# Decode attention: projection weights in runs of four rows, the head dimension ordered by ScalarE during the PSUM copy, the last tile's columns placed by TensorE

## The chip, the cores and the metric

The kernel runs on one core of one Trainium2 chip. The metric is the device time of one execution in microseconds (us). Medians are quoted with the number of runs. The runs are on several chips, so every kernel is compared with runs of the kernel before in the same rounds on the same chip. A ratio is the mean time of one kernel's runs over that of the other's runs of the same rounds, so it isn't quite the ratio of the medians that stand beside it. A profile is one execution; its span is about 1.8 us shorter than the time of the same run.

The engines are TensorE (PE in the profile, PEld for its weight loads), VectorE (DVE), ScalarE (ACT) and SyncE (SP), which issues the DMAs, all but three of 10 KB or less.

## The reference

One token of each of 8 sequences attends to a cache of 4096 keys in 32 heads of 128, and a small MLP runs on the doubly normalised input. Only the attention matters here:

```python
x = A_x                                      # [8, 1, 640] bf16
xn = _layernorm(x)
q = (xn @ wq)            # -> [b, h, 1, 128]
scores = einsum("bhqd,bhkd->bhqk", q, k_cache) * 128**-0.5
o = einsum("bhqk,bhkd->bhqd", softmax(scores), v_cache)
attention = o.reshape(8, 1, 4096) @ wo       # wo [4096, 640]
return x + attention + MLP(layernorm(xn))
```

The caches are 537 MB together; everything else is about 15 MB.

## The kernel before

The work is cut into 64 tiles: a quad of 4 heads of one sequence. A tile needs 4 MB of keys (K) and 4 MB of values (V). Two K and two V buffers are filled in turn by one DMA queue. For each tile VectorE computes three quarters of q·K (multiply L558, fold L562, reduce L565, each twice), TensorE with ScalarE the rest. The softmax runs once per group of two tiles, except in the last group, where it runs per tile. Then TensorE multiplies with V into `PV_ps`, ScalarE copies that from PSUM to SBUF (`E_sb`, "the eviction"), TensorE turns it into columns (`OT_ps`), VectorE divides by the row sums and puts the columns where the projection wants them ("the placement"), and TensorE projects with `wo_sb`.

`wo_sb` holds `RW` consecutive rows of the projection weights in each partition. The larger `RW`, the longer the pieces that the DMA reads, but the head dimension must then be put into another order, and a column must be cut into `RW` blocks of partitions that VectorE moves to other partitions. `RW` is 2 before. TensorE makes the order by reading V with stride 2.

```python
RW, PB = 2, P // 2
...
wov = wo_sb[:, :, :].rearrange("p (y r) n -> p y (r n)", r=RW)
...
def vcols(t):
    return KV_sb[:, NK + t % NV, :].rearrange("p (j q r) -> p j r q", q=PB, r=RW)
...
def wo_rows(src):                                   # pieces of RW rows: 2560 bytes
    return src.rearrange("(y p r) n -> p y (r n)", p=P, r=RW)
... # values(t): the products with V, 32 matmuls of 128x512
r = e.matmul(PV_ps[32 * ct:32 * ct + HT * 4, t % 2, :], P_sb[:, i, m, :, :]...,
             vv[:, 4 * m:4 * m + 4, :, :], start=(q == 0), stop=(q == wide - 1))
... # the eviction: contiguous on both sides (L649)
e.activation(E_sb[:, k, 0:n], PV_ps[:, k, 0:n], ACT.Copy)
... # finish(g): the placement, 4 operations of 64x4 per group (L679)
for x in range(RW):
    for r in range(RW):
        q = slice(r * PB, (r + 1) * PB)
        i = e.tensor_tensor(dst[x * PB:(x + 1) * PB, r::RW, b0:b0 + GT],
              OT_ps...[q, x::RW, :], rinv_sb[q, g % 2, :]...[:, x::RW, :], ALU.mult)
...
def pe_keep(e, n):   # n dummy matmuls that keep TensorE busy near the end
    ...
for pos, n in ((pvpos(T - 2) + 0.25, 2), (pvpos(T - 1) + 0.075, 4), (pvpos(T - 1) + 0.115, 3), (pvpos(T - 1) + 0.2, 1)):
    add("pe", pos, lambda e, n=n: pe_keep(e, n), ...)
```

The last tile's V comes in three pieces (half, quarter, quarter), so that its product can start before all of it is there.

## Time and profile before

| | before |
|---|---|
| time, median of 3 runs | 1290.28 us (1290.17 to 1290.29) |
| span of the profiled run | 1288.2 us |
| load queue busy | 99.8% of 16 engines |
| VectorE busy | 89% |
| one 4 MB load lands after the one before | 9.71 us |
| VectorE waits for K | 51.8 us in all |

From the page of the profiled run: the busy time of each engine, the load queue, and the chain of work that ended last, by engine.

```profile
PE 641.0 (50%) x7931; PEld 403.3 (31%) x7934; DVE 1141.1 (89%) x680; ACT 496.9 (39%) x1243; POOL 0.2 (0%) x4
...
q1 hardware_dynamic: 21440, 551.80, 99.8%
...
DMA 77%; DVE 11%; PE 8%; issue 4%; ACT 0%; SPq 0%; DVEq 0%
```

The queue is never empty and the chain is DMA for three quarters of the span.

VectorE reaches the K of tile 4 10.4 us after it has landed. It gains on the DMA (149.2 us per eight tiles against 157.1, from the starts of L558 and the landings), has caught up at tile 13, and from there on waits for K once per group. This is the timeline of VectorE at the end of a group in the steady part (start us, us, engine, line, operation, names, shapes, count, and the idle time before with its cause):

```profile
920.04 0.68 DVE L679 TENSOR_TENSOR oTn_sb<-C_ps,rinv_sb 64x4 bf16<-64x4 f32 x4
921.72 3.36 DVE L558 TENSOR_TENSOR Y_sb<-KV_sb,qbc_sb 128x6144 bf16<-128x6144 bf16 x1 [0.99 <-DMA KV_sb<-in_A_k_cache_dram]
```

The four placements take 0.68 us together, and the wait behind them is the slack. The eviction is cheap (groups by shape; busy us and mean ns of one, then the idle time before):

```profile
L649 ACT ACTIVATE E_sb<-PV_ps 128x512 bf16<-128x512 f32 x64 | 38.2, 597 | 306.2 <-PE PV_ps L630 306.2
L649 ACT ACTIVATE E_sb<-PV_ps 128x128 bf16<-128x128 f32 x1 | 0.3, 278 | 2.0 <-PE PV_ps L640 2.0
```

The end of the chain, in order of time (start us, us, what):

```profile
1267.14 15.92 DMA KV_sb<-in_A_v_cache_dram
...
1283.11 0.74 PE PV_ps L640 x32
...
1283.86 0.29 ACT E_sb L649
...
1284.20 0.19 PE C_ps L662
...
1285.15 0.73 PE TR_ps L691 x8
...
1285.90 0.48 DVE out_sb L805
```

The last piece of V lands at 1283.06 us, and only 5.1 us of work follow it. All the other work of the last two tiles is done by then.

### The profile page before, as it was taken

Reading aid. Unit: us, or ns where it says so; the run is one execution under the profiler, and the core shown is the slowest. Engines: PE = TensorE matmul, PEld = TensorE weight load, DVE = VectorE, ACT = ScalarE, POOL = GpSimd, SP = SyncE. Lnnn points to the kernel's source line nnn. Section 1 sums busy time; section 2 is a strip of 40 time slices with the busy share of each in tenths; the row PEclk is TensorE's granted clock in tenths of the full one; section 3 lists DMA queues with packets and bytes.
Section 4 is the critical chain, followed back from the end, with each engine's and each line's share of the span. In section 5 each row is a group of like instructions: output and inputs, shape, how many; then the busy total and the mean of one; then the engine's idle time right before and its main releaser. Section 6 shows DMA issues by size and latency. Waiting matters only on the chain.

```text
span 1288.2 us, 19951 instructions
## 1 busy us (share of the span) xinstructions
PE 641.0 (50%) x7931; PEld 403.3 (31%) x7934; DVE 1141.1 (89%) x680; ACT 496.9 (39%) x1243; POOL 0.2 (0%) x4
## 2 busy tenths in 40 slices
PE   2754454444554455454455444544544554455456
PEld 1433233223333233232233232332332332333332
DVE  4989999998898898898988988988989989889895
ACT  1444344334344234343243342443432443433432
POOL 0000000000000000000000000000000000000000
PEclk9755555565555655656656556555565556655556
DMA  9999999999999999999999999999999999999998
GB/s 408 423 427 429 437 429 432 429 429 433 431 431 432 432 428 434 429 433 429 431 431 432 430 428 436 429 433 429 430 432 432 430 435 429 428 434 430 432 430 351
DMA packets 21488, 552.00 MB, mean 429 GB/s; under 512 B 2313, under 2 KB 2401, under 8 KB 4450
## 3 DMA queue, kind: packets, MB, share of 16 engines
q1 hardware_dynamic: 21440, 551.80, 99.8%
q8 instruction: 8, 0.13, 0.0%
q14 instruction: 6, 0.05, 0.0%
q10 hardware_dynamic: 34, 0.02, 0.0%
HBM read 551.80 MB, written 0.01 MB: 428 GB/s over the span
## 4 chain that ended last, share of the span: by engine, by line
DMA 77%; DVE 11%; PE 8%; issue 4%; ACT 0%; SPq 0%; DVEq 0%
DMA KV_sb<-in_A_v_cache_dram 73%; PE PV_ps L630 7%; DVE Y_sb L558 6%; DVE Y_sb L562 3%; DMA KV_sb<-in_A_k_cache_dram 2%; DVE S_sb L565 2%; DMA KV_sb<-in_A_wq_dram 2%; DVE oTn_sb L679 0%; DVE M_sb L577 0%; PE CH_ps L579 0%; SPq L372 0%; DVE rinv_sb L611 0%; PE PV_ps L640 0%; PE TR_ps L691 0%; PE TR_ps L470 0%
## 5 line engine op out<-in xcount | busy, mean ns | idle before, releaser
L558 DVE TENSOR_TENSOR Y_sb<-KV_sb,qbc_sb 128x6144 bf16<-128x6144 bf16 x128 | 429.0, 3352 | 67.0 <-DMA KV_sb<-in_A_k_cache_dram 51.8
L565 DVE TENSOR_REDUCE S_sb<-Y_sb 128x48 f32<-128x3072 bf16 x128 | 429.2, 3353 | 4.4
L529 ACT ACTIVATE KT_sb<-TR_ps 128x1024 bf16<-128x1024 bf16 x256 | 254.6, 1021 | 232.5 <-PE TR_ps L526 231.1
L630 PE MATMUL PV_ps<-KV_sb,P_sb 128*16 128x512 bf16 x2040 | 222.0, 609 | 132.0 <-DMA KV_sb<-in_A_v_cache_dram 132.0
L526 PE MATMUL TR_ps<-ident_bf,KV_sb 128*128 128x128 bf16 x2048 | 248.3, 308 | 53.1 <-DMA KV_sb<-in_A_k_cache_dram 52.6
L562 DVE TENSOR_TENSOR Y_sb<-Y_sb 128x3072 bf16<-128x3072 bf16 x128 | 225.0, 1758 | 4.4
L526 PEld LDWEIGHTS TR_ps<-ident_bf,KV_sb 128*128 128x128 bf16 x2048 | 200.4, 141 | 63.3 <-DMA KV_sb<-in_A_k_cache_dram 57.5
L536 PE MATMUL S_ps<-qk_sb,KT_sb 128*128 128x4 bf16 x2048 | 98.0, 170 | 140.3 <-ACT KT_sb L529 138.3
L649 ACT ACTIVATE E_sb<-PV_ps 128x512 bf16<-128x512 f32 (+1 forms) x65 | 38.5, 592 | 308.2 <-PE PV_ps L630 306.2
L536 PEld LDWEIGHTS S_ps<-qk_sb,KT_sb 128*128 128x128 bf16 x2048 | 85.9, 109 | 171.7 <-ACT KT_sb L529 171.7
L630 PEld LDWEIGHTS PV_ps<-KV_sb,P_sb 128*16 128x16 bf16 x2040 | 60.7, 120 | 246.3 <-DMA KV_sb<-in_A_v_cache_dram 137.2
L597 ACT ACTIVATE P_sb<-S_sb,NB_sb 32x128 bf16<-32x128 f32 x256 | 101.9, 398 | 3.8
L655 PE MATMUL C_ps<-sel_bf,E_sb 128*128 128x4 bf16 x256 | 16.9, 172 | 159.7 <-DVE rinv_sb L611 133.7
L591 ACT ACTIVATE NB_sb<-CH_ps 128x2 f32<-128x2 f32 (+1 forms) x33 | 5.7, 172 | 177.1 <-PE CH_ps L587 177.1
L579 PE MATMUL CH_ps<-ident_f,M_sb 128*2 128x128 f32 (+1 forms) x33 | 12.2, 369 | 117.7 <-DVE M_sb L577 117.7
L655 PEld LDWEIGHTS C_ps<-sel_bf,E_sb 128*128 128x128 bf16 x256 | 11.4, 103 | 189.4 <-DVE rinv_sb L611 136.4
L546 ACT ACTIVATE S_sb<-S_ps 32x32 f32<-32x32 f32 x256 | 48.2, 188 | 32.0 <-PE S_ps L536 29.8
L597 ACT ACTIVATION_READ_ACCUMULATOR P_sb<-S_sb,NB_sb 32x1 f32 x256 | 47.1, 184 | 0.0
L579 PEld LDWEIGHTS CH_ps<-ident_f,M_sb 128*2 128x2 f32 (+1 forms) x33 | 2.6, 80 | 120.6 <-DVE M_sb L577 120.6
L673 DVE MEMSET oTn_sb<- 128x16 uint32 x30 | 2.2, 72 | 31.1 <-PE ACC_ps L704 31.1
L581 DVE TENSOR_REDUCE M_sb<-CH_ps 2x4 f32<-2x128 f32 (+1 forms) x33 | 9.2, 279 | 15.9 <-PE CH_ps L579 15.9
L704 PE MATMUL ACC_ps<-oTn_sb,wo_sb 128*128 128x8 bf16 x600 | 20.8, 169 | 0.0
(96 smaller groups left out, 212.8 us busy)
## 6 DMA issues: line engine op xcount, KB each, us to landing
KV_sb<-in_A_k_cache_dram SPq DMA_DIRECT2D x64, 4096.0 KB, 26.8
KV_sb<-in_A_v_cache_dram SPq DMA_DIRECT2D x63, 4096.0 KB, 35.2
KV_sb<-in_A_wq_dram SPq DMA_DIRECT2D x1, 5120.0 KB, 23.8
wo_sb<-in_A_wo_dram SPq DMA_DIRECT2D x7, 640.0 KB, 30.8
KV_sb<-in_B_w_dram SPq DMA_DIRECT2D x1, 2160.0 KB, 39.0
w_sb<-in_B_w_dram SPq DMA_DIRECT2D x1, 2080.0 KB, 43.8
KV_sb<-in_A_v_cache_dram SPq DMA_DIRECT2D x1, 2048.0 KB, 12.7
KV_sb<-in_A_v_cache_dram SPq DMA_DIRECT2D x2, 1024.0 KB, 15.1
```

Source lines behind the costliest of these rows:

```text
L526: r = e.transpose(TR_ps[:, it.box[0], jj * P:(jj + 1) * P], kv[:, n * BK + jj, :], ident_bf[:, :])
L529: add("act", t - 0.59 + 0.12 * n, lambda e: e.activation(KT_sb[:, m % NS, :, :].rearrange("p a b -> p (a b)"), TR_ps[:, it.box[0], :], ACT ...
L536: r = e.matmul(S_ps[:, c:c + HT], KT_sb[:, m % NS, jj, :], qk_sb[:, :, i], start=True, stop=True)
L546: r = e.activation(S_sb[s, g % SR, i, 0:JP], S_ps[s, 0:JP * HT].rearrange("p (j a) -> p j a", a=HT)[:, :, a], ACT.Copy)
L558: return e.tensor_tensor(y, kv[:, j0:j1, :], qbc_sb[:, g % 2, i, :][:, None, :].to_broadcast([P, nj, P]), ALU.mult)
L562: lambda e, y=y, y2=y2: e.tensor_tensor(y2, y[:, :, 0:P // 2], y[:, :, P // 2:P], ALU.add),
L565: lambda e, y2=y2, j0=j0, j1=j1: e.tensor_reduce(S_sb[:, g % SR, i, j0:j1], y2, AX.X, ALU.add),
L597: r = e.activation(P_sb[s, i, :, a, :], S_sb[s, g % SR, i, :].rearrange("p (m c) -> p m c", c=4), ACT.Exp, bias=NB_sb[s, g % 2, i:i + 1], ...
L630: r = e.matmul(PV_ps[32 * ct:32 * ct + HT * 4, t % 2, :], P_sb[:, i, m, :, :].rearrange("p a c -> p (a c)"), vv[:, 4 * m:4 * m + 4, :, :], ...
L649: add("act", pos, lambda e: e.activation(E_sb[:, k, 0:n], PV_ps[:, k, 0:n], ACT.Copy), R=[("PV", k)] + ["wo"] * (t % GT and not last), W=[ ...
L655: r = e.matmul(OT_i, E_sb[:, t % 2, c * P:(c + 1) * P], sel_bf[:, c:HT * 4:4], start=(c == 0), stop=(c == 3 and not last))
L704: r = e.matmul(ACC_ps[:, c * B:(c + 1) * B], wo_sb[:, a, c * P:(c + 1) * P], oTn_sb[:, a, :], start=False, stop=False, skip_group_check=True)
```

## The change

The intent is longer DMA pieces (5120 bytes instead of 2560) and unit stride for TensorE's reads of V. The last quad keeps `LW = 2`, so that the work behind the last load stays short. ScalarE makes the order in the eviction. VectorE then has 4 x 4 = 16 placements of 32x2 per group in the first seven quads, 4 in the last. For the very last tile TensorE itself puts the columns into the right partitions with small matmuls, and VectorE needs one operation. Cut to its core:

```diff
-    RW, PB = 2, P // 2
+    RW, LW = 4, 2
-    def wo_rows(src):
-        return src.rearrange("(y p r) n -> p y (r n)", p=P, r=RW)
+    def wo_rows(src, w):
+        return src.rearrange("(y p r) n -> p y (r n)", p=P, r=w)
     ... # RW for the first seven loads, LW for the last quad's two
-            vv = vcols(t)
+            vv = vview(t)                      # unit stride
     ...
+            def ordered(ap, w):
+                return ap.rearrange("p (c r q) -> p c q r", r=w, q=P // w)
+            def natural(ap, w):
+                return ap.rearrange("p (c q r) -> p c q r", r=w, q=P // w)
             def evac(pos, k, n):
-                ... e.activation(E_sb[:, k, 0:n], PV_ps[:, k, 0:n], ACT.Copy)
+                if t < T - B:
+                    fn = lambda e: e.activation(ordered(E_sb[:, k, 0:n], RW), natural(PV_ps[:, k, 0:n], RW), ACT.Copy)
+                else:
+                    fn = lambda e: e.activation(ordered(E_sb[:, k, 0:n], LW), natural(PV_ps[:, k, 0:n], LW), ACT.Copy)
     ...
+            def pe_ex_last(e, k, sel, cs):     # the last tile: 16 and 4 small matmuls
+                ...
+                            i = e.matmul(OTL_ps[x * n:(x + 1) * n, r::LW], E_sb[:, k, c * P + r * n:c * P + (r + 1) * n],
+                                         sel[:, x * cs + c::LW * cs], ...)
     ...
-            def norm(e):
-                for x in range(RW):
-                    for r in range(RW): ...    # 4 of 64x4
+            def place(e, dst, w, gs):
+                for x in range(w):
+                    for r in range(w): ...     # 16 of 32x2 with w = RW, 4 with w = LW
+            ... # the last tile: one operation of 128x4 from OTL_ps, with rinvL_sb
```

Both views in the eviction walk in the order c, q, r. So PSUM is read contiguously, and the writes into `E_sb` are single bf16 elements, 32 elements apart with `RW` and 64 apart with `LW`. The change also moves the start of ScalarE's rolled loop (the part of its program that repeats every eight tiles) from 2.27 to 2.21.

More of the change, by code (lines that the diff above doesn't have):

```diff
@@ L287, in bass_parallel_sum__gqa_block_cached__mixer_channel_mlp__decode_kernel @@
         rinv_sb = sb("rinv_sb", [P, 2, HT * GT], F32)
+        rinvL_sb = sb("rinvL_sb", [P, HT // LW], F32)
         oTn_sb = sb("oTn_sb", [P, HT, B], BF)
@@ L300, in bass_parallel_sum__gqa_block_cached__mixer_channel_mlp__decode_kernel @@
         wov = wo_sb[:, :, :].rearrange("p (y r) n -> p y (r n)", r=RW)
+        wovL = wo_sb[:, :, :].rearrange("p (y r) n -> p y (r n)", r=LW)
         M1T_ps = CH_ps[0:GT, 0:P]
@@ L304, in bass_parallel_sum__gqa_block_cached__mixer_channel_mlp__decode_kernel @@
         RS_ps = C2_ps[:, 8:8 + HT * GT]
+        OTL_ps = C2_ps[:, 16:16 + HT]
+        RSL_ps = C2_ps[:, 20:20 + HT // LW]
         QB_ps = CH_ps[:, 2 * P:2 * P + GT * P]
@@ L327, in vview @@
             return KV_sb[:, NK + t % NV, :].rearrange("p (j d) -> p j d", d=P)
-        def vcols(t):
-            return KV_sb[:, NK + t % NV, :].rearrange("p (j q r) -> p j r q", q=PB, r=RW)
         def span(i, n):
@@ L401, in bass_parallel_sum__gqa_block_cached__mixer_channel_mlp__decode_kernel @@
         ld(-95.0, w2_sb[0:FR, FC, :], B_w2[FC * P:F, :], ["w2r"], "w2r")
-        def wo_rows(src):
-            return src.rearrange("(y p r) n -> p y (r n)", p=P, r=RW)
+        def wo_rows(src, w):
+            return src.rearrange("(y p r) n -> p y (r n)", p=P, r=w)
         for hg in range(NG - 1):
             ld(hg * B + 3.65, wov,
-               lambda hg=hg: wo_rows(A_wo[span(hg, HT * P), :]), ["wo"],
+               lambda hg=hg: wo_rows(A_wo[span(hg, HT * P), :], RW), ["wo"],
                "wo")
-        wo_last = wo_rows(A_wo[(H - HT) * P:H * P, :])
-        ld(T - 0.1, wov[:, 0:HT // RW - 1, :], wo_last[:, 0:HT // RW - 1, :], ["wo"], "wo")
-        ld(T - 0.09, wov[:, HT // RW - 1, :], wo_last[:, HT // RW - 1, :], ["wo3"], "wo3")
+        wo_last = wo_rows(A_wo[(H - HT) * P:H * P, :], LW)
+        ld(T - 0.1, wovL[:, 0:HT // LW - 1, :], wo_last[:, 0:HT // LW - 1, :], ["wo"], "wo")
+        ld(T - 0.09, wovL[:, HT // LW - 1, :], wo_last[:, HT // LW - 1, :], ["wo3"], "wo3")
         def layernorm(n, pos, src, src_res, dst, dst_res):
@@ L606, in rowsum @@
         def rowsum(g):
-            rp = pvpos(g * GT) + 0.21 if g < NGRP - 1 else pvpos(T - 1) - 0.04
+            rp = pvpos(g * GT) + 0.21
             add("pe", rp, lambda e: e.matmul(RS_ps, ones_f[:, :], rs_sb[:, :, :].rearrange("p a g -> p (a g)"),
@@ L612, in rowsum, with pe_rsl @@
                 R=["RS"], W=[("rinv", g % 2)], X=["C2"])
+            if g < NGRP - 1:
+                return
+            def pe_rsl(e):
+                n = P // LW
+                for x in range(LW):
+                    r = e.matmul(RSL_ps[x * n:(x + 1) * n, :], ones_f[:, 0:n], rs_sb[:, x::LW, GT - 1],
+                                 start=True, stop=True)
+                return r
+            add("pe", rp + .002, pe_rsl, R=[("rs", GT - 1), "ones"], W=["RSL"], X=["C2"])
+            add("dve", rp + .012, lambda e: e.reciprocal(rinvL_sb[:, :], RSL_ps), R=["RSL"], W=["rinvL"], X=["C2"])
         for g in range(NGRP):
@@ L631, in pe_pv @@
                                      P_sb[:, i, m, :, :].rearrange("p a c -> p (a c)"),
-                                     vv[:, 4 * m:4 * m + 4, :, :],
+                                     vv[:, 4 * m:4 * m + 4, :],
                                      start=(q == 0), stop=(q == wide - 1))
@@ L640, in pe_pv_last @@
                             r = e.matmul(PV_ps[32 * ct:32 * ct + HT, 1 - t % 2, 0:P], P_sb[:, i, m, :, c],
-                                         vv[:, 4 * m + c, :, :], start=(q == wide and c == 0),
+                                         vv[:, 4 * m + c, :], start=(q == wide and c == 0),
                                          stop=(q == NQ - 1 and c == 3))
@@ L646, in values @@
                     R=[("V", t % NV, q), ("Pt", i)], W=[("PV", k)], X=[("PVb", k)])
+            def ordered(ap, w):
+                return ap.rearrange("p (c r q) -> p c q r", r=w, q=P // w)
+            def natural(ap, w):
+                return ap.rearrange("p (c q r) -> p c q r", r=w, q=P // w)
             def evac(pos, k, n):
-                add("act", pos, lambda e: e.activation(E_sb[:, k, 0:n], PV_ps[:, k, 0:n], ACT.Copy),
+                if t < T - B:
+                    fn = lambda e: e.activation(ordered(E_sb[:, k, 0:n], RW), natural(PV_ps[:, k, 0:n], RW), ACT.Copy)
+                else:
+                    fn = lambda e: e.activation(ordered(E_sb[:, k, 0:n], LW), natural(PV_ps[:, k, 0:n], LW), ACT.Copy)
+                add("act", pos, fn,
                     R=[("PV", k)] + ["wo"] * (t % GT and not last), W=[("E", k)], X=[("PVb", k)])
@@ L655, in pe_ex @@
                     r = e.matmul(OT_i, E_sb[:, t % 2, c * P:(c + 1) * P], sel_bf[:, c:HT * 4:4],
-                                 start=(c == 0), stop=(c == 3 and not last))
+                                 start=(c == 0), stop=(c == 3))
                 return r
-            evac(p0 + (0.13 if last else 0.22), t % 2, 4 * P)
-            add("pe", p0 + (0.14 if last else 0.28), pe_ex, R=[("E", t % 2), "sel"], W=["OT"], X=["C2"])
-            if last:
+            def pe_ex_last(e, k, sel, cs):
+                n = P // LW
+                for r in range(LW):
+                    for c in range(cs):
+                        for x in range(LW):
+                            i = e.matmul(OTL_ps[x * n:(x + 1) * n, r::LW], E_sb[:, k, c * P + r * n:c * P + (r + 1) * n],
+                                         sel[:, x * cs + c::LW * cs], start=(cs > 1 and r == c == 0), stop=(cs == 1),
+                                         skip_group_check=True)
+                return i
+            evac(p0 + (0.13 if last else 0.22), t % 2, 4 * P)
+            if not last:
+                add("pe", p0 + 0.28, pe_ex, R=[("E", t % 2), "sel"], W=["OT"], X=["C2"])
+            else:
+                add("pe", p0 + 0.14, lambda e: pe_ex_last(e, t % 2, sel_bf, 4), R=[("E", t % 2), "sel"], W=["OTL"],
+                    X=["C2"])
                 evac(p0 + 0.27, 1 - t % 2, P)
-                add("pe", p0 + 0.28, lambda e: e.matmul(OT_i, E_sb[:, 1 - t % 2, 0:P], sel2_bf[:, :], start=False,
-                                                       stop=True), R=[("E", 1 - t % 2), "sel"], W=["OT"], X=["C2"])
+                add("pe", p0 + 0.28, lambda e: pe_ex_last(e, 1 - t % 2, sel2_bf, 1), R=[("E", 1 - t % 2), "sel"],
+                    W=["OTL"], X=["C2"])
         def finish(g):
@@ L669, in finish @@
             tail = g >= NGRP - GPH
-            res = "oL" if tail else "oTn"
-            dst = oL_sb if tail else oTn_sb
+            last = g == NGRP - 1
             if g <= NGRP - GPH + 1:
                 add("dve", np_ - 0.004, lambda e: e.memset(oTn_sb[:, :, :], 0.0), W=["oTn", "oTn0"])
-            def norm(e):
-                for x in range(RW):
-                    for r in range(RW):
-                        q = slice(r * PB, (r + 1) * PB)
+            def place(e, dst, w, gs):
+                n = P // w
+                for x in range(w):
+                    for r in range(w):
+                        q = slice(r * n, (r + 1) * n)
                         i = e.tensor_tensor(
-                            dst[x * PB:(x + 1) * PB, r::RW, b0:b0 + GT],
-                            OT_ps.rearrange("p (a g) -> p a g", a=HT)[q, x::RW, :],
-                            rinv_sb[q, g % 2, :].rearrange("p (a g) -> p a g", a=HT)[:, x::RW, :], ALU.mult)
-                return i
-            add("dve", np_, norm, R=["OT", ("rinv", g % 2), "oTn0"], W=[res], X=["C2"])
+                            dst[x * n:(x + 1) * n, r::w, b0:b0 + gs],
+                            OT_ps.rearrange("p (a g) -> p a g", a=HT)[q, x::w, 0:gs],
+                            rinv_sb[q, g % 2, :].rearrange("p (a g) -> p a g", a=HT)[:, x::w, 0:gs], ALU.mult)
+                return i
+            if not tail:
+                add("dve", np_, lambda e: place(e, oTn_sb, RW, GT), R=["OT", ("rinv", g % 2), "oTn0"], W=["oTn"], X=["C2"])
+            elif not last:
+                add("dve", np_, lambda e: place(e, oL_sb, LW, GT), R=["OT", ("rinv", g % 2), "oTn0"], W=["oL"], X=["C2"])
+            else:
+                add("dve", np_ - 1, lambda e: place(e, oL_sb, LW, GT - 1), R=["OT", ("rinv", g % 2)], W=["oL"], X=["C2"])
+                add("dve", np_, lambda e: e.tensor_tensor(
+                    oL_sb[:, :, B - 1].rearrange("p (y r) -> p y r", r=LW),
+                    OTL_ps.rearrange("p (y r) -> p y r", r=LW),
+                    rinvL_sb[:, :][:, :, None].to_broadcast([P, HT // LW, LW]), ALU.mult),
+                    R=["OTL", "rinvL"], W=["oL"], X=["C2"])
         w = D // 2
@@ L694, in bass_parallel_sum__gqa_block_cached__mixer_channel_mlp__decode_kernel @@
         LAST = pvpos(T - 1) + 0.4
-        add("pe", LAST, lambda e: pe_last(e, range(HT - RW)), R=["wo", "oL", "base_ps"], X=[("TR", 0)])
-        add("pe", LAST + 0.01, lambda e: pe_last(e, range(HT - RW, HT)), R=["wo3"], W=["fin"], X=[("TR", 0)])
+        add("pe", LAST, lambda e: pe_last(e, range(HT - LW)), R=["wo", "oL", "base_ps"], X=[("TR", 0)])
+        add("pe", LAST + 0.01, lambda e: pe_last(e, range(HT - LW, HT)), R=["wo3"], W=["fin"], X=[("TR", 0)])
         def project(g):
@@ L830, in _ @@
         def _(e):
-            sch.emit_rolled("act", e, sems, 2.27, B)
+            sch.emit_rolled("act", e, sems, 2.21, B)
 _INS = ['A_x', 'A_k_cache', 'A_v_cache', 'A_wq', 'A_wo', 'B_x', 'B_w1', 'B_b1', 'B_w2', 'B_b2']
```

## The prediction

> **What bounds the kernel now.** DMA, from about 100 us on. The queue table gives the load queue 99.8% of 16 engines. Each 4 MB K or V load lands 9.71 us after the one before (issues and landings), so two tiles take 38.86 us; a projection-weight load adds 1.64 us once per eight tiles: 157.1 us per eight. VectorE is close behind (89% busy). Its timeline shows that it starts late, about 10 us behind the K landings at 105 us, and does two tiles in 37.19 us until it has caught up near 272 us (plus 0.38 us once per eight tiles, at the loop's turn: 149.1 us per eight). After that it waits 1.5 us per two tiles for K (51.8 us in all). So its slack is 8.0 us per eight tiles.
>
> **What the change does.**
> 1. Weight loads: 2560-byte packets took 105 ns in the mean, 8192-byte ones 317, 32768-byte ones 1218. An estimate from these for 5120 bytes is 200 ns; 8 packets per engine in place of 16 saves under 0.1 us per load, 0.5 us over seven.
> 2. TensorE reads V with unit stride instead of 2; ScalarE orders columns while it evicts. 32 value matmuls take 3.62 us[...], and the eviction 0.60 us for 512 columns; I expect both unchanged, and neither is critical.
> 3. VectorE's placement becomes 16 operations of 32x2 per two tiles instead of 4 of 64x4. The four start 0.167 to 0.179 us apart, nearly all fixed cost. [...] no overlap inside the four. Estimate: 0.170 us each, +2.04 us per two tiles, for 28 groups (the last head quad keeps 4).
> 4. Tail: the last tile's four placements (0.70 us) become one (about 0.17), its one placing matmul becomes four (+0.1): -0.4 us.
>
> **What is critical.** Step 3 costs 8.2 us per eight tiles against 8.0 of slack. VectorE then never catches up: it stays 11 to 13 us behind K through the kernel. The DMA doesn't starve (K is issued 17 us ahead without lag, so some 4 us remain), but the start lag is carried to the end. Summing VectorE's measured spacings, it begins the last K tile 8 us after its landing instead of at once (the last quad wins back some 4). The last softmax's small matmuls stand in front of the value matmuls of tile 62 on TensorE's queue, so both last value passes come after the last V landing instead of during it. Adding up that chain (18.4 us to the bias matmul, 3.4 values, 1.4, 4.2 for the last tile, 4.0 end) gives +5.4 us; less 0.4 in the tail already in it.
>
> **Prediction.** 1295.3 us, range 1289.6 to 1298.0. Faster by over 2%: 0.005; within 2%: 0.975; slower by over 2%: 0.02.
>
> **What would show it.** Placement groups of about 2.75 us; VectorE's total wait for K from 52 to under 10 us; busy near 93%; K issued about 4 to 6 us before its turn, landings still 9.71 us apart; weight loads landing 1.55 us after their predecessor; the last bias matmul at 1280 us instead of 1272.8; the last wait on V gone from the chain, VectorE over most of it; at the end one placement of 0.17 us.
>
> **What would make it wrong.** The sum is steep in the cost of one placement: at 0.152 us VectorE catches up, the tail gain stands alone, and the time is 1289.4; at 0.18 us it is 1299. If the ordered eviction or a changed TensorE order stalls VectorE further, the DMA starves too.

The sum came to 1290.28 (before) + 5.4 - 0.4 = 1295.3 us. The 0.170 us for one placement is the estimate from the spacing in the trace before; that a 32x2 costs nearly what a 64x4 does was measured afterwards (154 ns against 161, medians of L715 after and L679 before).

## More of the kernel before

The DMA bounds this kernel. VectorE follows closely: two of its waits (total us, times, longest):

```profile
DVE Y_sb L558 <- DMA KV_sb<-in_A_k_cache_dram: 51.8, 34, 2.4
...
DVE M_sb L577 <- DVE S_sb L565: 2.0, 7, 0.5
```

## The result, and the profile after

| | before (6 runs) | after (6 runs) |
|---|---|---|
| time, median | 1290.55 us (1290.17 to 1291.27) | 1298.87 us (1298.03 to 1299.27) |
| ratio | | 1.0063 (95%: 1.005 to 1.0076) |
| span of the profiled run | 1288.2 us | 1297.2 us |

The kernel became 8.3 us slower, which is within 2%. The prediction had the direction and the class right, but its range ended at 1298.0.

The same three lines of the page after the change:

```profile
PE 634.2 (49%) x7953; PEld 403.1 (31%) x7953; DVE 1189.6 (92%) x1018; ACT 615.4 (47%) x1243; POOL 0.2 (0%) x4
...
q1 hardware_dynamic: 20544, 551.80, 99.0%
...
DVE 67%; issue 26%; DMA 4%; PE 2%; ACT 1%; DVEq 0%; SPq 0%
```

VectorE has taken the chain over from the DMA, although the queue is still 99% busy. And ScalarE has 118.5 us more work (615.4 - 496.9) with the same number of instructions, nearly all of it in the evictions below (64 x 1.83). VectorE's wait for K is nearly gone, and its wait on L577 is no longer listed:

```profile
DVE Y_sb L558 <- DMA KV_sb<-in_A_k_cache_dram: 4.7, 2, 2.4
```

VectorE at the end of a group:

```profile
928.63 2.69 DVE L715 TENSOR_TENSOR oTn_sb<-C_ps,rinv_sb 32x2 bf16<-32x2 f32 x16
931.36 3.36 DVE L558 TENSOR_TENSOR Y_sb<-KV_sb,qbc_sb 128x6144 bf16<-128x6144 bf16 x1
```

Sixteen placements take 2.69 us, 2.01 more than the four, and K has long been there when they end. VectorE now needs 156.82 us per eight tiles against the DMA's 157.05. It hardly gains: it is 12.4 us behind K's landing at tile 4 and still 10.0 behind at tile 56. In the last quad, with four placements per group, it regains some and begins the last K tile at 1258.92 us, 5.4 us after its landing. The loads land 9.71 to 9.72 us apart as before; a projection-weight load lands 1.57 to 1.59 us after its predecessor, where it took 1.60 to 1.66.

VectorE's start on the last K tile, first before the change, where it waits for the landing, then after it, where K landed at 1253.51 us:

```profile
1253.78 3.36 DVE L558 TENSOR_TENSOR Y_sb<-KV_sb,qbc_sb 128x6144 bf16<-128x6144 bf16 x1 [0.67 <-DMA KV_sb<-in_A_k_cache_dram]
...
1258.92 3.34 DVE L558 TENSOR_TENSOR Y_sb<-KV_sb,qbc_sb 128x6144 bf16<-128x6144 bf16 x1
```

The evictions:

```profile
L669 ACT ACTIVATE E_sb<-PV_ps 128x512 bf16<-128x512 f32 x56 | 136.2, 2431 | 150.0 <-PE PV_ps L642 150.0
L671 ACT ACTIVATE E_sb<-PV_ps 128x512 bf16<-128x512 f32 x8 | 19.7, 2465 | 20.8 <-PE PV_ps L642 20.8
L671 ACT ACTIVATE E_sb<-PV_ps 128x128 bf16<-128x128 f32 x1 | 0.7, 740 | 1.5 <-PE PV_ps L652 1.5
```

One takes 2431 ns where it took 597. In the steady part this delays nobody who matters: e2_two_rows below has the slow evictions too, and there VectorE waits for K as long as before (51.9 us). But the end of the chain now looks like this:

```profile
1277.29 3.55 PE PV_ps L642 x32
...
1280.86 2.46 ACT E_sb L671
...
1283.70 1.81 PE PV_ps L642 x13
1285.51 1.82 PE ACC_ps L846 x4
1287.33 0.99 PE PV_ps L642 x7
...
1288.35 2.45 ACT E_sb L671
...
1292.26 0.75 ACT E_sb L671
...
1293.37 0.19 DVE oL_sb L726
...
1293.60 1.25 PE TR_ps L737 x8
...
1294.87 0.48 DVE out_sb L851
```

Three things are to be seen. The products of tile 62 end only at 1280.84, and those of tile 63, whose first half of V has been there since 1278.82, begin at 1283.63. The last piece of V lands at 1283.77, so the products of a whole tile stand behind it, where before there was only the last quarter of one. Three slow evictions stand in the chain (2.46, 2.45 and 0.75 us); the first runs while V still lands, but it holds up the products of tile 63. And the matmuls are slow: the 16 of tile 63 with the four dummies (1.82 us by themselves) and the next 8 take 4.62 us, the last projection (L737) 1.25 us where it took 0.73. That last point is the granted clock, the share of its full speed at which TensorE was allowed to run. These windows are 3.41 us each (window, its length, busy time and count of PE, PEld, DVE, ACT and POOL, then the granted PE clock, the DMA share and GB/s). Before:

```profile
1272.48:1275.89 3.41, 2.94 (x36) 1.16 (x40) 0.57 (x5) 2.13 (x9) 0.00 (x0) 0.50 1.03 437
1275.89:1279.30 3.41, 2.57 (x36) 0.94 (x29) 0.21 (x1) 0.60 (x1) 0.00 (x0) 1.00 0.97 404
...
1282.71:1286.12 3.41, 1.56 (x41) 0.85 (x41) 0.86 (x5) 0.50 (x2) 0.00 (x0) 1.00 0.18 67
```

After:

```profile
1279.16:1282.57 3.41, 3.41 (x24) 1.22 (x16) 0.24 (x2) 2.11 (x3) 0.00 (x0) 0.50 0.90 369
1282.57:1285.98 3.41, 2.57 (x23) 0.85 (x23) 0.66 (x4) 0.74 (x1) 0.00 (x0) 0.50 0.15 59
1285.98:1289.39 3.41, 3.41 (x15) 0.56 (x13) 0.00 (x0) 1.04 (x1) 0.00 (x0) 0.50 0.00 0
1289.39:1292.80 3.41, 1.55 (x50) 0.90 (x49) 0.00 (x0) 1.94 (x2) 0.00 (x0) 1.00 0.02 5
```

Before, the full clock is there from 1275.9 us to the end of the last projection, 10.2 us. After, it is there for 3.4 us, and the last projection comes too late for it.

### The profile page after: what moved, and what is told of

Its sections match the earlier page's. It is cut to its first block, busy times and chain, and to the rows that moved or that the text cites. A ratio compares the mean times of both kernels' runs of the same rounds, so it can differ in the third digit from the quotient of the medians.

```text
span 1297.2 us, 20331 instructions
## 1 busy us (share of the span) xinstructions
PE 634.2 (49%) x7953; PEld 403.1 (31%) x7953; DVE 1189.6 (92%) x1018; ACT 615.4 (47%) x1243; POOL 0.2 (0%) x4
## 4 chain that ended last, share of the span: by engine, by line
DVE 67%; issue 26%; DMA 4%; PE 2%; ACT 1%; DVEq 0%; SPq 0%
DVE Y_sb L558 32%; DVE Y_sb L562 17%; DVE S_sb L565 11%; DVE oTn_sb L715 5%; DMA KV_sb<-in_A_k_cache_dram 2%; DMA KV_sb<-in_A_wq_dram 2%; DVE M_sb L577 1%; PE CH_ps L579 1%; PE PV_ps L642 0%; DVE rinv_sb L611 0%; ACT E_sb L671 0%; DVEq L178 0%; DVE M_sb L581 0%; PE ACC_ps L846 0%; DVE oTn_sb L708 0%
## 5 line engine op out<-in xcount | busy, mean ns | idle before, releaser
L642 PE MATMUL PV_ps<-KV_sb,P_sb 128*16 128x512 bf16 x2040 | 222.1, 612 | 0.0
L669 ACT ACTIVATE E_sb<-PV_ps 128x512 bf16<-128x512 f32 x56 | 136.2, 2431 | 150.0 <-PE PV_ps L642 150.0
L642 PEld LDWEIGHTS PV_ps<-KV_sb,P_sb 128*16 128x16 bf16 x2040 | 62.2, 122 | 107.3 <-issue 104.9
L715 DVE TENSOR_TENSOR oTn_sb<-C_ps,rinv_sb 32x2 bf16<-32x2 f32 x448 | 69.6, 155 | 6.7
L671 ACT ACTIVATE E_sb<-PV_ps 128x512 bf16<-128x512 f32 (+1 forms) x9 | 20.5, 2273 | 22.3 <-PE PV_ps L642 20.8
```

The costliest lines, as they stand in the source:

```text
L669: fn = lambda e: e.activation(ordered(E_sb[:, k, 0:n], RW), natural(PV_ps[:, k, 0:n], RW), ACT.Copy)
L715: i = e.tensor_tensor(dst[x * n:(x + 1) * n, r::w, b0:b0 + gs], OT_ps.rearrange("p (a g) -> p a g", a=HT)[q, x::w, 0:gs], rinv_sb[q, g % 2 ...
```

## The experiments

The theory after the result had two parts. *Lag*: the sixteen placements use up VectorE's slack, so that it begins the last K tile late; this delays the products of the last two tiles. *Eviction*: the reordered write is slow, and three evictions lie in the chain at the end. That they also cost TensorE its clock was a guess of mine, which no run shows. The rivals: the lag alone explains everything; or the eviction alone does; or the unit-stride V reads, the weight loads or the last tile's new matmuls have a cost of their own.

The comparison with the reference passed for every kernel, also for the three that compute a wrong result. It therefore isn't sensitive to the order of the head dimension, and that the other kernels keep the right order rests on the reading of the code.

| run | what it is | median us | before, same rounds | ratio (95%) |
|---|---|---|---|---|
| e1_walk | after, eviction writes contiguously | 1292.43 | 1290.45 | 1.0021 (1.0007 to 1.0035) |
| e2_two_rows | after, runs of two rows | 1294.31 | 1290.45 | 1.0032 (1.0018 to 1.0045) |
| e3_both | both of these | 1289.81 | 1290.45 | 0.9997 (0.9984 to 1.0011) |
| e4_sixteen | before, 16 placements | 1292.88 | 1290.45 | 1.0019 (1.0005 to 1.0032) |
| e5_rows_only | before, only the loads changed | 1289.99 | 1290.35 | 0.9996 (0.9982 to 1.001) |
| e6_two_quads | e1, the last two quads with two rows | 1291.0 | 1290.35 | 1.0002 (0.9989 to 1.0016) |
| e7_runs | after, eviction in short runs | 1292.63 | 1290.35 | one run |
| e8_warm | after, more dummies | 1296.99 | 1290.35 | 1.0052 (1.0038 to 1.0066) |
| e9_best | e6, more dummies | 1291.98 | 1290.52 | 1.0008 (0.9994 to 1.0022) |
| e10_two_rows_warm | e3, more dummies | 1289.85 | 1290.52 | 1.0001 (0.9988 to 1.0015) |
| e11_before_warm | before, more dummies | 1290.25 | 1290.52 | 0.9998 (0.9985 to 1.0012) |
| e12_strided_warm | e2, more dummies | 1293.66 | 1290.29 | 1.0022 (1.0009 to 1.0036) |
| e13_steps | after, eviction in three other steps | 1294.39 | 1290.29 | one run |

A timed kernel had five runs. e7 and e13 have one each, in an unknown state; only the duration of their evictions is used.

### e1_walk: the same order, the stride on the reading side

```diff
             def ordered(ap, w):
-                return ap.rearrange("p (c r q) -> p c q r", r=w, q=P // w)
+                return ap.rearrange("p (c r q) -> p c r q", r=w, q=P // w)
             def natural(ap, w):
-                return ap.rearrange("p (c q r) -> p c q r", r=w, q=P // w)
+                return ap.rearrange("p (c q r) -> p c r q", r=w, q=P // w)
```

The same element goes to the same place; only the order of the walk differs. Now `E_sb` is written contiguously and PSUM is read with a stride of four or two fp32 elements.

> The changed kernel with one thing undone: the eviction walks the columns so that it writes E_sb contiguously and reads PSUM with a step of 4 (last quad 2) floats; same values, same placements. Theory (two causes: VectorE's lag from 12 more placements, and three slow evictions on the chain at the end): each 512-column eviction 0.60 us instead of 2.43, the 128-column one 0.29 instead of 0.74; VectorE still begins the last K tile 5.4 us after its landing; time 1294.2 us (1293 to 1295). Rival 1 (lag alone costs the 8.3 us, evictions are hidden): 1298 to 1299. Rival 2 (the slow evictions alone cost it, by holding ScalarE and the PSUM buffers, and make VectorE late as well): 1290, lag gone.

The eviction is as fast as before the change, here with the stride of four; with the stride of two (L671) it took 597 ns too:

```profile
L669 ACT ACTIVATE E_sb<-PV_ps 128x512 bf16<-128x512 f32 x56 | 33.4, 597 | 147.1 <-PE PV_ps L642 147.1
```

and TensorE's 16 products of tile 63 and its last projection run at the full clock, which the profiled run had from 1280.9 us on (timeline):

```profile
1282.08 1.04 PE L642 MATMUL PV_ps<-KV_sb,P_sb 128*16 128x512 bf16 x16
...
1287.58 0.71 PE L737 MATMUL TR_ps<-wo_sb,oL_sb 128*8 128x320 bf16 x8 [0.27 <-DVE oL_sb L726]
```

The lag is still there (5.5 us at the last tile). The time is 6.4 us below that of after (1298.87 - 1292.43, each median from its own rounds; before differs by 0.1 between them). I had expected 1294.2 (1293 to 1295), so the size was a miss. Two of the five runs did take 1294.2 and 1294.6; they have no profile, so what they had in common isn't known. The half clock, which costs 2.6 us at the end of after, would fit, but their mean clocks on record (0.573 and 0.572 against 0.570 to 0.574) don't tell.

### e2_two_rows: runs of two rows, the slow eviction kept

```diff
-    RW, LW = 4, 2
+    RW, LW = 2, 2
```

> The changed kernel with runs of two rows in every quad, so 4 placements per two tiles as before; the slow strided-write eviction stays. Theory: VectorE catches up as before the change (lag at the last K tile 0 to 0.1 us), evictions 2.4 us; only the last two evictions lie on the chain: 1.2 us after hiding for the first, 0.45 for the second, less 0.45 for the single placement: 1291.9 us (1291 to 1293). Rival 1 (lag alone): 1289.9. Rival 2 (evictions alone): 1297 to 1299.

The lag is gone (0.0 us at the last tile, and 51.9 us of waits for K as before the change), but the kernel is 3.9 us slower than before, 2.4 us more than I had expected. So the lag isn't needed for a loss. The runs spread from 1292.6 to 1295.2. The profiled one was the fastest; it had the full clock from 1277.9 us on. All three evictions of the last two tiles are slow here too (start, us), the third 0.74 us at 1286.35:

```profile
1277.07 2.45 ACT L671 ACTIVATE E_sb<-PV_ps 128x512 bf16<-128x512 f32 x1 [2.45 <-PE PV_ps L642]
1282.44 2.44 ACT L671 ACTIVATE E_sb<-PV_ps 128x512 bf16<-128x512 f32 x1 [2.92 <-PE PV_ps L642]
```

### e3_both: both undone

The edits of e1_walk and e2_two_rows together. What stays of the change is the unit-stride read of V and the new work for the last tile.

> The changed kernel with both undone: runs of two rows everywhere and the contiguous-write eviction. What is left of the change is unit-stride reading of V and the last tile's placing on TensorE. Theory: 1290.1 us, 0.45 below the kernel before of the same rounds: one placement of 0.18 us at the end instead of four (0.70), three more small matmuls (+0.1). A third cause hidden in what is left would show as more than 1291.

A hit. The median is 0.64 us below that of before, the interval includes 1. The unit-stride reads cost and bring nothing: L642 took 612 ns for a product in the profile after, L630 609 before. The last tile's single placement took the 0.17 us that I had predicted in place of 0.70.

With e3 as the base, e1 adds 2.6 us (the lag), e2 adds 4.5 us (the eviction), and after adds 9.0 (taken against the before of each one's rounds: +8.3 and -0.6). Both together cost about 1.8 us more than their sum. In the profiled runs alone the spans give 2.8, 3.0 and 9.3 us, and there the chains show where the excess comes from: 2.6 us are the half clock of after, which neither e1 nor e2 had in its profile. The rest lies in tile 62's eviction. Without the lag the wait for V hides part of it: in e2 it brings the next eviction to 1282.44 from 1281.41 in e3, 1.0 us, where with the lag it costs all of its 1.86.

### e4_sixteen: only the sixteen placements

The kernel before, with each 64x4 placement of the first seven quads cut into four of 32x2. The result is the same.

```diff
-            def norm(e):
+            def norm(e, n=PB // 2 if g < NGRP - GPH else PB):
                 for x in range(RW):
-                    for r in range(RW):
-                        q = slice(r * PB, (r + 1) * PB)
-                        i = e.tensor_tensor(...)
+                    for y in range(0, HT // RW, n * HT // RW // PB):
+                        for r in range(RW):
+                            for h in range(0, PB, n):
+                                z = y + n * HT // RW // PB
+                                q = slice(r * PB + h, r * PB + h + n)
+                                i = e.tensor_tensor(...)
```

> The kernel BEFORE, with one thing added: each of its four 64x4 placements is cut into four 32x2 ones (16 per two tiles[...]) in all but the last quad. Same values, weights in runs of two, old fast eviction. Theory: the placements alone make the lag: 16 take 2.7 us, VectorE waits for K under 10 us in all, and it begins the last K tile 5 to 6 us after its landing; time 1293.8 us (1292.5 to 1295). Rival (lag comes from something else in the change, such as ScalarE being busier): lag 0 to 1 us, time 1290.5.

A hit: +2.4 us, with no other part of the change in it. The wait for K falls from 51.8 to the same value as after:

```profile
DVE Y_sb L558 <- DMA KV_sb<-in_A_k_cache_dram: 4.8, 2, 2.4
```

VectorE needs 156.82 us per eight tiles here too and begins the last K tile 5.1 us after its landing. The sixteen placements alone make the lag. The 2.0 us of waits on L577 that the kernel before has (seven times, once per turn of VectorE's rolled loop) are also gone here, as they are in after; they are there again in e2 and e3. So they go with the sixteen placements. Why isn't known.

### e5_rows_only: only the weight loads

The kernel before with four-row runs in the first seven weight loads and nothing that fits them (a wrong result).

```diff
-        def wo_rows(src):
-            return src.rearrange("(y p r) n -> p y (r n)", p=P, r=RW)
+        def wo_rows(src, w=RW):
+            return src.rearrange("(y p r) n -> p y (r n)", p=P, r=w)
+        wov4 = wo_sb[:, :, :].rearrange("p (y r) n -> p y (r n)", r=4)
         for hg in range(NG - 1):
-            ld(hg * B + 3.65, wov, lambda hg=hg: wo_rows(A_wo[span(hg, HT * P), :]), ["wo"], "wo")
+            ld(hg * B + 3.65, wov4, lambda hg=hg: wo_rows(A_wo[span(hg, HT * P), :], 4), ["wo"], "wo")
```

> The kernel BEFORE with only the seven projection-weight loads changed to runs of four rows; nothing is reordered for it, so its result is wrong on purpose. Theory: 5120-byte packets take about 200 ns; a weight load lands 1.58 us after its predecessor instead of 1.64; 0.4 us less over seven loads, 1290.1 us. Rival (the packet size matters more, or less, than the packet times say): over 1 us less, or nothing.

A hit. The loads land 1.53 to 1.59 us after their predecessors instead of 1.60 to 1.66, and the median falls by 0.36 us, less than the interval can tell from nothing. This is all that the longer pieces can bring: seven loads of 0.66 MB out of 552 MB.

### e6_two_quads: the lag along the way, not at the end

e1_walk with two-row runs, and so four placements, in the last two quads instead of one.

```diff
-    SR = 2
+    SR, LQ = 2, 2
-        for hg in range(NG - 1):
+        for hg in range(NG - LQ):
             ... # RW
+        for hg in range(NG - LQ, NG - 1):
+            ... # LW
-                if t < T - B:
+                if t < T - LQ * B:
-            if not tail:
+            if g < NGRP - LQ * GPH:
                 ... # place(e, oTn_sb, RW, GT)
+            elif not tail:
+                ... # place(e, oTn_sb, LW, GT)
```

> The changed kernel with the contiguous-write eviction, and runs of four rows in the first six head quads only (the last two keep runs of two, 4 placements). Theory: what costs is VectorE's lag at the end, not its lag on the way; eight pairs of tiles with 1.7 to 2 us of slack each take back the 10 to 11 us, lag at the last K tile 0 to 0.3 us, six of seven weight loads keep their saving: 1289.4 us, 0.3 to 0.4 below the kernel with runs of two everywhere. Rival (the lag on the way costs DMA time): K landings more than 9.72 us apart and a time above 1290.5.

The lag was 10.8 us at tile 48, 4.1 at tile 56, 0.6 at tile 60 and 0.0 at tile 63, while the loads still landed 9.72 us apart. So a lag of 11 us along the way doesn't starve the DMA (after, e1 and e4 have the same lag and keep their landings); only what is left of it at the end costs. But the time was 1.6 us above what I had expected, where the rival had put it. Two landings were late (9.91 us after the one before at 1038 us, 10.40 at 1128), together 0.9 us, and TensorE had the half clock until 1282.8 us in the profiled run. Late landings at these two times came again in e9_best and in no other profile (after 225 us the others have only single ones, 0.2 us late at most); their cause is open.

### e7_runs: eviction writes in runs of two and four

After, with another (wrong) order: pairs of adjacent elements, each pair 128 elements from the last, in the first seven quads, and runs of four in the last.

```diff
             def ordered(ap, w):
-                return ap.rearrange("p (c r q) -> p c q r", r=w, q=P // w)
+                z = 8 // w
+                return ap.rearrange("p (r q z) -> p q r z", r=w, z=z)
             def natural(ap, w):
-                return ap.rearrange("p (c q r) -> p c q r", r=w, q=P // w)
+                z = 8 // w
+                return ap.rearrange("p (q r z) -> p q r z", r=w, z=z)
```

> The changed kernel with another column order in the eviction, so a wrong result on purpose: it writes runs of 2 elements (4 bytes) in the first seven quads and runs of 4 elements (8 bytes) in the last, PSUM read contiguously as in the changed kernel. It measures the eviction by itself. Theory (the cost is per separate run written, about 4.4 ns per lone 2-byte element, and not per step of the address): 512 columns take about 1.3 us with runs of 2 and 0.7 us or less with runs of 4. Rival (any strided write costs 4.4 ns per element): 2.4 us in both.

The 4.4 ns of the theory come from the two sizes after the change: (2431 - 740) / 384 ns per element, with about 175 ns fixed. The rival was wrong, and so was the theory for pairs; for runs of four it was right:

```profile
L671 ACT ACTIVATE E_sb<-PV_ps 128x512 bf16<-128x512 f32 x56 | 34.8, 622 | 151.7 <-PE PV_ps L642 151.7
L673 ACT ACTIVATE E_sb<-PV_ps 128x512 bf16<-128x512 f32 x8 | 4.8, 597 | 20.7 <-PE PV_ps L642 20.7
```

Pairs cost 622 ns, almost nothing over 597. The slow case is single elements (2431 ns).

### e13_steps: single elements at three steps

Run last, to tell what about single elements is slow. After, with single elements again, 2 elements apart in the first seven quads, 4 apart in the last, and 8 apart for the last tile's 128x128 (a wrong result).

```diff
             def ordered(ap, w):
-                return ap.rearrange("p (c r q) -> p c q r", r=w, q=P // w)
+                z = {4: 2, 2: 4}[w] if ap.shape[-1] == 4 * P else 8
+                return ap.rearrange("p (q z) -> p z q", z=z)
             def natural(ap, w):
-                return ap.rearrange("p (c q r) -> p c q r", r=w, q=P // w)
+                z = {4: 2, 2: 4}[w] if ap.shape[-1] == 4 * P else 8
+                return ap.rearrange("p (z q) -> p z q", z=z)
```

> The kernel after the change with other write steps in the eviction (a wrong result on purpose; PSUM is read contiguously as after the change). The first seven quads write single bf16 elements 2 elements (4 bytes) apart, the last quad 4 elements (8 bytes) apart, the one 128x128 eviction of the last tile 8 elements (16 bytes) apart. Theory [...]: the 128x512 evictions take about 0.6 us in all quads[...]; the 128x128 one[...] about 0.74 us as after the change. Rival (what counts is that each write is a lone 2 bytes, wherever the next one goes): about 2.43 us in all quads, and 0.74 us for the 128x128 one. A third outcome, a cost that rises with the step: 0.6 us or a little over at 4 bytes, something between at 8 bytes.

The third outcome came:

```profile
L671 ACT ACTIVATE E_sb<-PV_ps 128x512 bf16<-128x512 f32 x56 | 41.5, 742 | 152.2 <-PE PV_ps L642 152.2
L673 ACT ACTIVATE E_sb<-PV_ps 128x512 bf16<-128x512 f32 x8 | 10.5, 1308 | 20.4 <-PE PV_ps L642 20.4
L673 ACT ACTIVATE E_sb<-PV_ps 128x128 bf16<-128x128 f32 x1 | 0.7, 736 | 1.5 <-PE PV_ps L652 1.5
```

The passages cut from the expectation were the reason for its theory; it isn't shown, and for the 128x512 copies the theory was wrong (742 and 1308 ns, not about 600). What the runs show is the time by step. A 128x512 copy of single elements took 742 ns at a step of 2 elements, 1308 at 4, 2431 at 32 and 2465 at 64 (the last two after the change); a 128x128 copy took 736 ns at 8 and 740 at 64. Taking off the 175 ns of e7_runs, an estimate, leaves 1.1 ns per element at a step of 2, 2.2 at 4 and 4.4 at 8, at 32 and (4.5) at 64: it doubles from 2 to 4 and from 4 to 8, and the larger steps tried cost no more. The pairs of e7, 128 elements apart, took 622 ns, 1.7 ns per pair by the same reckoning. Why pairs are nearly free and single elements are not, no run shows.

### e8_warm: more dummies after the change

```diff
-        for pos, n in ((pvpos(T - 2) + 0.25, 2), (pvpos(T - 1) + 0.075, 4), (pvpos(T - 1) + 0.115, 3), ...):
+        for pos, n in ((pvpos(T - 2) + 0.25, 4), (pvpos(T - 1) + 0.075, 4), (pvpos(T - 1) + 0.115, 6), ...):
```

> The changed kernel with five more dummy matmuls that fill TensorE's waits for the two slow evictions at the end (4 and 6 in place of 2 and 3). Theory: of the changed kernel's loss a third part of about 2.5 us is TensorE's granted clock[...], the last tile's 24 value matmuls and 4 dummies take 2.6 us instead of 4.7, the final eight matmuls 0.7 instead of 1.2: 1296.3 us (1295.5 to 1297.5). Rival (evictions and lag are all): no change or slower by the added matmuls, 1298.9 to 1300.

A hit in time: 1.9 us less than after (1.7 when each is taken against the before of its own rounds), and no run of one lies among the other's. In the profiled run the clock was full from 1280.3 to 1290.6 us, and the 16 products of tile 63 took 1.04 us instead of 1.88:

```profile
1277.76 3.16 PE L642 MATMUL PV_ps<-KV_sb,P_sb 128*16 128x512 bf16 x32
...
1281.61 0.82 PE L846 MATMUL ACC_ps<-zeros_bf 128*128 128x512 bf16 x3 [0.16 <-issue]
...
1283.74 1.04 PE L642 MATMUL PV_ps<-KV_sb,P_sb 128*16 128x512 bf16 x16
```

The last projection was again late for it (1.23 us). But these lines also show that the added dummies didn't bring the full clock: it came at 1280.3 us, and the first dummy on record ran at 1281.61. Whether they kept it is not shown. So that the 1.9 us are the clock, and that waiting for slow evictions loses it, is my guess and not shown.

What brought it isn't shown, but what stood before it can be counted. In the clock records of before and after, every stretch at full or half clock is a whole multiple of 3.413 us (97 and 73 of them). This grid lies differently from run to run: modulo 3.413 us from the start of the span, the clock became full at 2.7 us before (1275.9), 2.6 after (1289.4), 0.9 in e1 (1280.9), 1.3 in e2 (1277.9) and 0.3 in e8 (1280.3). All fifteen profiles together have 98 whole grid windows at half clock after 1255 us. Counting in each only the time in matmuls of 512 columns (value products and dummies), the 22 windows that the full clock followed had 2.57 us or more, the 76 others 2.64 or less. The time in all matmuls tells less: 2.94 us on record in a window before were followed by the full clock, 3.41 us in one after by the half clock (the first line of each table of windows above). Tile 62's products alone last about one window (3.2 to 3.6 us). In e1 and e8 one window held 3.41 and 2.58 us of them; after the change the grid cut them in two, and the windows from 1275.8, 1279.2 and 1282.6 us had 1.97, 2.64 and 2.40. Of the three only the last has a recorded wait for an eviction in it.

### e9_best, e10_two_rows_warm, e11_before_warm, e12_strided_warm: is there a version that beats both?

e9 is e6, e10 is e3 and e11 is the kernel before, each with six dummies instead of two after tile 62's products:

```diff
-        for pos, n in ((pvpos(T - 2) + 0.25, 2), ...
+        for pos, n in ((pvpos(T - 2) + 0.25, 6), ...
```

e12 is e2 with the dummies of e8.

> The kernel with contiguous-write evictions and runs of four rows in the first six head quads, with four more dummy matmuls (6 instead of 2) ahead of the last tile's values. The same kernel without them missed its forecast (1291.0 instead of 1289.4) with the granted clock at half until 1282.8 us. Theory: that clock was the miss; [...] the time is 1289.4 us (1289.0 to 1290.2). Rival (runs of four rows cost something at the end): 1290.5 to 1291.5 again, with the clock full.

> Runs of two rows in all quads, contiguous-write evictions (the kernel that took 1289.81 with runs from 1289.66 to 1291.01), with the same four more dummy matmuls. Theory: the median stays near 1289.8 (the profiled run had full clock from 1276 us already) and the run at 1291.0 goes away; 0.3 to 0.4 above the kernel with six quads in runs of four.

> The kernel BEFORE with the same four more dummy matmuls and nothing else: a control. Theory: 1290.3 us, within 0.3 of the kernel before, since its profile shows full clock from 1275.9 us. If it is 1 us faster, what the other two kernels gain belongs to the dummies and not to the placing on TensorE.

> Runs of two rows everywhere with the slow strided-write eviction (the kernel that was forecast at 1291.9 and took 1294.31, with runs from 1292.61 to 1295.18, the fast one being the profiled one, at full clock from 1277.9 us), with five more dummy matmuls that fill TensorE's waits for the slow evictions. Theory: the miss of 2 us was granted clock in the runs that were not profiled; [...] most runs come to 1292.3 to 1293.0. Rival (the slow evictions cost these 2 us in another way): the median stays at 1294 to 1295.

e9 missed (1291.98 against 1289.4): the profiled run had the full clock from 1276.8 us, but lost landings again (10.15 us apart at 1038 us, 10.23 at 1128, 9.86 at 1167). e10 missed in part: its median, 1289.85, is e3's, but two of five runs took 1291.6 and 1292.1 (so did one of the nine runs of before beside it, 1292.09), so the dummies don't take the slow runs away. e11, the control, was a hit: the dummies do nothing for the kernel before. e12 gained 0.65 us on e2 (0.5 with each against its own before), less than expected; in its profiled run the half clock lasted until 1281.9 us in spite of the dummies. So the dummies don't bring the clock reliably. No version beats the kernel before by more than the noise; e3_both is its equal.

## Why the prediction was right or wrong

**Right: the mechanism of the lag.** "Step 3 costs 8.2 us per eight tiles against 8.0 of slack." It costs 8.04 (4 x 2.01), and e4 shows that it alone makes the lag and +2.4 us. The placements into `oTn_sb` start 0.159 to 0.178 us apart, take 0.146 to 0.167 us each and don't overlap (at least 13 ns lie between the end of one and the start of the next, as before the change). "The DMA doesn't starve" was right (after, e1, e4). "Both last value passes come after the last V landing" was right for tile 63 alone; that of tile 62 ended at 1280.84 us, before the last piece of V landed.

**Right: the small gains.** 0.36 us for the loads (e5; predicted 0.5; the 5120-byte packets took 199 ns in the mean after the change, estimated 200), one placement of 0.17 us in the tail.

**Wrong in size: the lag at the end.** Predicted 8 us, measured 5.4. The mis-sized term is 0.38 us per eight tiles at the loop's turn, which I kept and which vanished: 149.16 - 0.38 + 8.04 = 156.82, exactly the pace measured. So VectorE gained 0.2 us per eight tiles on the DMA's 157.05 where I had it lose 0.2. The lag therefore cost 2.6 us (e1 against e3) and not the 5.4 that I had added up for it.

**Wrong: the step that failed.** "the eviction 0.60 us for 512 columns; I expect both unchanged, and neither is critical." The value products were unchanged. The eviction took 2.43 us, because it writes lone 2-byte elements 32 apart (0.60 with contiguous writes, e1), and at the end it was critical, for a reason that stands in the prediction itself: if both value passes lie on the chain, so do their evictions. I carried 0.60 over from a copy with contiguous writes to one with scattered writes, without a number for it. Here is the predicted chain beside the measured ones (us; e1 is after with the fast eviction; the prediction doesn't say where its last two terms part, so compare their sum):

| stretch | predicted | after | e1_walk |
|---|---|---|---|
| VectorE begins the last K tile at | 1261.8 | 1258.9 | 1259.1 |
| to the last bias matmul (L587, part of the last softmax) | 18.4 | 18.1 | 18.1 |
| to the eviction of tile 62 | 3.4 | 3.8 | 3.8 |
| to the first product of tile 63 | 1.4 | 2.8 | 1.0 |
| to the eviction of tile 63 | 4.2 | 4.7 | 2.6 |
| to the end of the span | 4.0 | 8.9 | 6.0 |
| end | 1293.2 | 1297.2 | 1290.7 |

Against e1, the three evictions add 1.86 + 1.85 + 0.47 = 4.2 us, and the half clock adds about 2.1 in the stretch from tile 63's first product to its eviction and 0.5 in the last projection. This makes 6.8; the two spans differ by 6.5, because e1 came 0.2 us later to its last K tile.

That the forecast came within 3.6 us is luck: two errors of opposite sign. e1 is the kernel that I had reckoned with, lag and an eviction of 0.60 us, and it took 1292.43. With the lag sized right I would have missed by about 6 us.

**Wrong for having left it out: TensorE's clock at the end.** The prediction took its durations from the trace before, which had the full clock in the last 10 us, and has no term for the clock. After the change the half clock cost 2.6 us in the profiled run. The grid of 3.41 us lies differently from run to run (see e8_warm), so part of this may be chance; whether the waits for slow evictions cause any of it is not shown. Runs of one kernel differ by up to 2.6 us; the profiled runs of e2, e8 and e12 show the clock differing, but for the runs without a profile it is only argued that the clock makes this.

**Open.** Why the wait at the loop's turn goes with sixteen placements; why landings are late in the two kernels with two quads of two rows (e6, e9); what sets apart the slower runs of e1, e2 and e10; whether the added dummies of e8 work through the clock.

## What to carry to other kernels

Compare a fixed cost per period with the slack of the engine that pays it, and then ask what the engine still owes at the end: a lag of 11 us along the way was free here, 5.1 to 5.5 us at the last tile cost 2.4 to 2.6 (e4, e1). When a copy from PSUM reorders, put the stride on the reading side (597 ns here, e1), or write at least pairs of elements (622 ns, e7) and not lone ones (2431 ns); two swapped letters in the walk were worth 6.4 us with the lag and 4.5 without it. And take a duration over to the new kernel only if the access pattern on both sides is the same.
